# FNet layer with an MLP beside it on one Trainium2 core: bank-freeing work right behind each product, all else later, two sums of C per step, buffers and pools moved

## The chip, the cores and the metric

The kernel runs on one core of a Trainium2 chip. The metric is device time of one execution in microseconds (us). TensorE (PE) multiplies matrices into PSUM banks; VectorE (DVE) and ScalarE (ACT) read PSUM and do elementwise work; GpSimd (POOL) reduces over partitions and starts accumulating transfers; SyncE (SP) starts the other transfers. Each engine works through its own queue of instructions in order.

## The reference

```python
xn = (x - mean(x)) / sqrt(var(x) + 1e-5)                  # x: 2048 x 576, over the last axis
a, b = xn @ dft_hid_re.T, xn @ dft_hid_im.T
fnet = dft_seq_re @ a - dft_seq_im @ b                    # 2048 x 2048 by 2048 x 576, twice
mlp = maximum(xn @ w1, 0) @ w2                            # 576 x 4608 and 4608 x 576
out = x + fnet + mlp
```

## The kernel before

All matmuls are f16, with each f32 operand split into a high and a low f16 part (`split`, L182 on ScalarE for the high part and L183 on VectorE for the low one), so that one f32 product costs three f16 ones. Many products follow a seven-product scheme for a 2 x 2 block multiplication: sums and differences of blocks are formed first, then seven block products are accumulated and combined.

The hidden width of the MLP, 4608, is cut into nine blocks `b` of 512, and the 2048 rows into four groups `g` of 512. The main loop runs over the steps (b, g), numbered n from 2 to 35, blocks outermost. In a step the first matrix product of (b, g) stands among the seven parts of the second product (`mlp2`) of the step before. Blocks 0 and 1 compute the first product plainly (`mlp1_step`). From block 2 on (n = 8 to 35) it is itself done by seven products P1, P2, P6, P5, P7, P3, P4, for two pairs `first` and `second` (`pair_products`). They go through four PSUM banks: `u` of each pair, and `v` and `w` that both pairs share. P1, P6, P7 and P4 follow each other in `u`, P2 is in `v`, P5 and P3 are in `w`; P6, P7, P4 and P3 accumulate onto what their bank holds. Before the next product may write to a bank, `behind` must have read it: c11 = copy of P1 (ScalarE, L449), c11 += P2 (VectorE, L451), s1 = copy of P6 (ScalarE, L454), c22 = copy of P5 (ScalarE, L456), c22 += P7 (L458), r21 = P3 + s1 (L461). The rest makes the operands of the next step: `value` (relu on ScalarE, L444, and its low part on VectorE, L445), the relu of r21 (L462), four sums on VectorE (L463 to L468), and `end_hi` and `end_lo` (L474, L477), which split these sums and are called later through the list `ends`.

The seven parts of `mlp2` use two PSUM buffers. Parts 0, 2, 3 and 6 leave through a ScalarE copy into one of three sum buffers (`sumbufs`, L515), parts 1, 4 and 5 are added on VectorE (L517), and parts 1, 4, 5 and 6 go to memory by an accumulating transfer that GpSimd starts (L519, `spill`). In the last block two of these buffers' places are needed for the DFT's weights, so from its second step on three buffers lie in one w2 tile (`sums`).

Other work is spread over the steps by lists. `todo` holds the preparation of the next block's weights (`prepare_block`): load, largest value, scale, splits and sums, with empty entries as waits; `work()` takes one entry, and the code of a step calls it at fixed places. `passes` holds 65 entries that load a 512 KB piece of the sequence DFT matrix C (`first_c`, L863, into the one buffer `first`) and sum its absolute values on ScalarE (`sum_c`, L870), which gives the scales of C for the last stage. `tq` makes sums of x for the seven products (`sums_x`, L402 to L411), through a temporary `t` that shares the buffer `first`; so the passes begin after block 1.

After the loop, `dft1` multiplies by the hidden DFT for 16 row tiles (L989 and L999 into the banks `pd`, then L1009 to L1021), and the last stage multiplies by C (L1103), whose pieces are loaded by `load_c` (L1029) and split by `operand`. Their buffers lie in pools (`ra`, `tp`, `cs`, `cra`) that are stacked in the memory that the loop's pools have left, so where a pool stands decides which earlier tile it must wait for.

The program is written in a tile framework. It puts in the semaphores, and its scheduler sets the order of each engine's instructions from the order of the code, the dependences and its own estimate of when each can start. TensorE keeps the order of the code here; ScalarE, VectorE and the queues may take an instruction ahead of others that the code has earlier.

Of the kernel before, what the change touches and what calls it, by code (L numbers as in the profile page):

```python
# [9 lines left out]
F16 = mybir.dt.float16  # L10
# [21 lines left out]
KT = 5  # L32
# [17 lines left out]
def kernel(  # L50
# [340 lines left out]
    def sums_x(g):  # L391

        f = mlp.tile([P, 2, 2, GH], F32, tag="first", name=f"t{g}", bufs=1)
        tt = nc.vector.tensor_tensor
        for q, (head, tail) in enumerate((
            ((0, 1), (0, 0)), ((1, 1), None), ((1, 0), None), ((1, 1), (0, 1)),
        )):
            t = f[:, q % 2]
            h, l = halves(g, head)
            if tail:  # L400
                h2, l2 = halves(g, tail)
                tt(t, h, h2, ALU.subtract)  # L402
                tt(t, t, l2, ALU.subtract)
            else:
                tt(t, h, f[:, 1 - q % 2], ALU.subtract)
            tt(t, t, l, ALU.add)
# [8 lines left out]
    def pair_products(b, g, i):  # L415
# [26 lines left out]
        def value(q, src):  # L442
            hi, lo = h[:, 0, q], h[:, 1, q]
            nc.scalar.activation(hi, src, AF.Relu)  # L444
            stt(lo, src, 0.0, hi, ALU.max, ALU.subtract)  # L445

        def behind(n):
            if n == P1:
                nc.scalar.activation(c11, u, AF.Copy)  # L449
            elif n == P2:  # L450
                tt(c11, v, c11, ALU.add)  # L451
                value(A11, c11)
            elif n == P6:
                nc.scalar.activation(s1, u, AF.Copy)  # L454
            elif n == P5:
                nc.scalar.activation(c22, w, AF.Copy)  # L456
            elif n == P7:
                tt(c22, u, c22, ALU.add)  # L458
                value(A22, c22)
            elif n == P3:  # L460
                tt(r21, w, s1, ALU.add)  # L461
                nc.scalar.activation(r21, r21, AF.Relu)  # L462
                stt(s3, c11, 0.0, r21, ALU.max, ALU.subtract)  # L463
                stt(s1, c22, 0.0, r21, ALU.max, ALU.add)
                stt(s2, c22, 0.0, s3, ALU.max, ALU.subtract)
            elif n == P4:
                value(A12, u)
                stt(s4, u, 0.0, s2, ALU.max, ALU.subtract)  # L468
                ends.extend((end_hi, end_lo))

# [7 lines left out]

        def run(n):
            product(n)  # L480
            behind(n)

# [395 lines left out]
    for n in range(2, len(steps)):  # L878
# [13 lines left out]
        if b == 0 and g + 1 < NG:  # L892
            with tc.issue_after(order["lo"]):
                weave(stats([(g + 1) * TG + i for i in range(TG)]))
        if b == NB - 1 and g == 1:

            w = mlp.tile([P, 2, 7, EH], F16, tag="w2s", name="sums", bufs=4)
            w = w.rearrange("p n q e -> p (n q e)").bitcast(F32)
            sumbufs[:] = [
                w[:, k * 2 * EH : (k + 1) * 2 * EH].rearrange("p (c e) -> p c e", e=EH) for k in range(3)  # L900
            ]
        if b >= BB:
            first, second = (pair_products(b, g, i) for i in range(NQ))
            m = lambda q: mlp2(pb, pg, q)
            for k, (do, q) in enumerate((
                (first, P1), (first, P2), (m, 0), (first, P5), (first, P6), (m, 1), (second, P1),
                (first, P7), (m, 2), (second, P2), (first, P3), (first, P4), (m, 3), (second, P6),
                (m, 4), (second, P5), (second, P7), (m, 5), (m, 6), (second, P3), (second, P4),
            )):
                do(q)  # L910

                if k in (2, 4, 12, 14) and ends:
                    ends.pop(0)()
                for _ in range({2: 1, 3: 1, 5: 1, 8: 1, 9: 1, 12: 1, 13: 1, 16: 1, 18: 2}.get(k, 0)):
                    work()
                if n == 2 + NG * BB - 2 and k in (5, 9, 13, 18):
                    next(tq, None)
# [170 lines left out]
    for n, (p, kh) in enumerate(units):  # L1088
# [4 lines left out]
        for i, (q, rq, first, row, col) in enumerate(PRODUCTS):  # L1093
# [16 lines left out]
            if kh and i in (2, 4, 5, 6):  # L1110
# [3 lines left out]
                nc.sync.dma_start(out[rows, e], outs[p][:, h, e])  # L1114
    for pool in (op, cr[1], *rpool[:0:-1], cr[0], cs, tpool, rpool[0], psd, ps1):
        pool.release()
# [52 lines left out]
```

## Time and profile before

| | before |
|---|---|
| median of 3 runs (lowest, highest) | 1322.42 us (1322.38, 1323.62) |
| profiled execution, as timed | 1322.13 us |
| its span, first to last instruction | 1320.3 us |
| mean granted TensorE clock | 0.990 |
| TensorE busy | 1252.5 us (95%) |
| VectorE busy | 999.3 us (76%) |
| ScalarE busy | 726.7 us (55%) |
| GpSimd busy | 148.2 us (11%) |

The stages, read from the timeline: the start and block 0 until about 120 us, block 1 until 214, the seven-product blocks 2 to 8 from 214 to 863, the rest of `mlp2` until 875, `dft1` until about 990, and the product with C until the end. In a row of the timeline the first number is the start and the second the duration in us; a bracket at its end names how long the engine stood idle before it and what ended that. In a row of groups stand the count, the busy us, the mean ns of one, and the idle us before them. PEld is the loading of weights into TensorE. A tile is named by its buffer: `bank` is a product's PSUM bank, `acc` the place of c11 and c22, `s` the sums, `f` the piece of C.

### The profile page before, as it was taken

To read this page: it belongs to the slowest core of one execution; us is meant where nothing else is said; L and a number is where in the kernel's file an instruction comes from. 1 tells how busy PE (TensorE), PEld (TensorE's weight loads), DVE (VectorE), ACT (ScalarE), POOL (GpSimd) and SP (SyncE) were. 2 spreads that over 40 slices of the span, in tenths; PEclk is the share of its full clock that TensorE was granted. 3 is DMA by queue.
4 is the path that set the end of the run, shared out by engine and by line. 5 is a ranking of instruction groups with operands and counts; after the bars stand their busy time and mean duration, and the time that the engine had idled before them with its cause. 6 is when DMAs were issued, how large, how long until landed. Compare 5 with 4: busy or idle time off the path is not lost.

```text
span 1320.3 us, 25521 instructions
## 1 busy us (share of the span) xinstructions
PE 1252.5 (95%) x10396; PEld 994.1 (75%) x10396; DVE 999.3 (76%) x1879; ACT 726.7 (55%) x1218; POOL 148.2 (11%) x188
## 2 busy tenths in 40 slices
PE   8899998999999999899999898999999999999998
PEld 7665665877778778778778787877777777777777
DVE  8989996787677677668766767539667878878875
ACT  5745555586676667676665756435443433343332
POOL 2310021111111111121111121110000000000000
PEclk8899999999999999999999999999999999999999
DMA  5112354466656566475666665360005344343420
GB/s 220 41 64 74 110 92 91 82 134 150 146 133 145 128 143 135 110 167 126 132 140 156 145 139 120 61 127 17 1 27 190 112 148 138 108 150 113 147 82 19
DMA packets 60806, 150.75 MB, mean 114 GB/s; under 512 B 6288, under 2 KB 21136, under 8 KB 60688
## 3 DMA queue, kind: packets, MB, share of 16 engines
q1 hardware_dynamic: 42256, 111.36, 26.4%
q0 software_dynamic: 18432, 37.76, 19.3%
q8 instruction: 81, 1.33, 0.4%
q14 instruction: 37, 0.30, 0.1%
HBM read 101.91 MB, written 47.19 MB: 113 GB/s over the span
## 4 chain that ended last, share of the span: by engine, by line
PE 52%; DVE 10%; DMA 10%; issue 9%; ACT 8%; POOL 1%; SPq 0%; ACTq 0%; POOLq 0%; DVEq 0%
PE p L1103 24%; PE p L506 10%; PE bank L437 9%; PE pd L989 6%; DMA f<-in_cim_dram 4%; DMA f<-in_cre_dram 3%; ACT f L870 3%; PE p L310 2%; DVE w2s L183 2%; DMA raw_w<-in_w_dram 1%; POOL spill L519 1%; DMA c<-in_cre_dram 1%; ACT h L474 1%; DVE h L445 1%; ACT j L600 1%
## 5 line engine op out<-in xcount | busy, mean ns | idle before, releaser
L506 PE MATMUL p<-w2s,h 128*128 128x288 f16 x3024 | 409.9, 288 | 7.6 <-DVE acc L517 1.7
L506 PEld LDWEIGHTS <-h 128*128 128x128 f16 x3024 | 296.7, 98 | 87.4 <-issue 8.9
L1103 PE MATMUL p<-R,cs 128*128 128x288 f16 x2688 | 329.6, 286 | 1.5 <-DVE o L1109 1.5
L1103 PEld LDWEIGHTS <-cs 128*128 128x128 f16 x2688 | 263.0, 98 | 68.0 <-issue 1.7
L182 ACT ACTIVATE cs<-c,sc_c 128x1024 f16<-128x1024 f32 x112 | 128.4, 1148 | 196.1 <-PE p L1103 148.1
L437 PEld LDWEIGHTS <-w1buf 128*128 128x128 f16 x1600 | 157.5, 98 | 46.2 <-issue 24.5
L183 DVE SCALAR_TENSOR_TENSOR cs<-c,sc_c,cs 128x1024 f16<-128x1024 f32 x112 | 143.7, 1283 | 44.7 <-ACT cs L182 44.5
L437 PEld LDWEIGHTS <-dbuf 128*128 128x128 f16 x1200 | 117.3, 98 | 35.6 <-issue 20.2
L437 PE MATMUL bank<-acc,w1buf 128*128 128x256 f16 x768 | 106.1, 275 | 21.2 <-ACT s L454 19.6
L437 PE MATMUL bank<-xT,w1buf 128*128 128x256 f16 x832 | 110.9, 274 | 0.7 <-ACT acc L456 0.7
L989 PE MATMUL pd<-dbuf,xT 128*128 128x288 f16 x832 | 104.3, 286 | 1.7 <-DVE R L1018 1.5
L519 POOL DMA_DIRECT2D spill<-dbuf x74 | 64.7, 885 | 328.4 <-DVE dbuf L517 256.2
L989 PEld LDWEIGHTS <-xT 128*128 128x128 f16 x832 | 80.7, 98 | 25.7 <-issue 5.6
L437 PE MATMUL bank<-acc,dbuf 128*128 128x256 f16 x576 | 78.5, 272 | 17.9 <-ACT s L454 12.6
L870 ACT ACTIVATE f<-f 128x1024 f32<-128x1024 f32 x64 | 67.2, 1050 | 43.3 <-DMA f<-in_cim_dram 22.5
L477 DVE TENSOR_TENSOR h<-s,h 128x1024 f16<-128x1024 f32 x56 | 68.6, 1224 | 26.9 <-ACT h L474 26.7
L437 PE MATMUL bank<-xT,dbuf 128*128 128x256 f16 x624 | 82.3, 273 | 0.0
L474 ACT ACTIVATE h<-s 128x1024 f16<-128x1024 f32 x56 | 59.1, 1055 | 34.9 <-DVE s L468 34.9
L444 ACT ACTIVATE h<-acc 128x256 f16<-128x256 f32 x112 | 45.9, 410 | 51.6 <-DVE acc L458 33.6
L1109 DVE SCALAR_TENSOR_TENSOR o<-p,us_c,o 128x288 f32<-128x288 f32 x112 | 57.5, 514 | 19.9 <-PE p L1103 19.9
L515 ACT ACTIVATE dbuf<-p,c_ub 128x576 f32<-128x576 f32 x74 | 54.1, 732 | 22.6 <-PE p L506 17.6
L445 DVE SCALAR_TENSOR_TENSOR h<-acc,h 128x256 f16<-128x256 f32 x112 | 47.3, 422 | 23.1 <-ACT h L444 23.1
(158 smaller groups left out, 1543.1 us busy)
## 6 DMA issues: line engine op xcount, KB each, us to landing
spill<-dbuf POOLq DMA_DIRECT2D x74, 288.0 KB, 5.9
f<-in_cre_dram SPq DMA_DIRECT2D x32, 512.0 KB, 4.8
f<-in_cim_dram SPq DMA_DIRECT2D x32, 512.0 KB, 4.5
c<-in_cre_dram SPq DMA_DIRECT2D x32, 512.0 KB, 4.4
c<-in_cim_dram SPq DMA_DIRECT2D x32, 512.0 KB, 4.8
spill<-sum POOLq DMA_DIRECT2D x38, 288.0 KB, 5.5
raw_w<-in_w_dram SPq DMA_DIRECT2D x17, 640.0 KB, 5.7
raw_w<-in_w_dram SPq DMA_DIRECT2D x18, 576.0 KB, 4.0
```

Source lines behind the costliest of these rows:

```text
L182: nc.scalar.activation(hi, src, AF.Copy, scale=s)
L183: nc.vector.scalar_tensor_tensor(lo, src, s, hi, ALU.mult, ALU.subtract)
L437: nc.tensor.matmul(ps, l, r, start=first and m == 0, stop=m == len(todo) - 1, skip_group_check=not first,)
L445: stt(lo, src, 0.0, hi, ALU.max, ALU.subtract)
L474: order["s"] = nc.scalar.activation(hi_s, st[:, 1:], AF.Copy).ins
L477: order["lo"] = nc.vector.tensor_tensor(lo_s, st[:, 1:], hi_s, ALU.subtract).ins
L506: nc.tensor.matmul(ps[:, c], h[:, x, qa, c * P : (c + 1) * P], w[:, y, qb], start=first and i == 0 and j == 0, stop=i == NQ - 1 and j == 2 ...
L519: nc.gpsimd.dma_start(spill[g, row, col], o, accum_op=ALU.add)
L870: nc.scalar.activation(f, f, AF.Abs, scale=2.0**-10, accum_out=sums_c[:, n, q : q + 1])
L989: nc.tensor.matmul(ps[j], xT[g][:, kx, c * P : (c + 1) * P], dsp[j][:, hl, k], start=(t % 2 == 0 and n == 0), stop=(t % 2 == 1 and n == le ...
L1103: nc.tensor.matmul(ps, w[:, a, k], r[:, c, rq], start=first and k == 0 and j == 0, stop=k == HK - 1 and j == 2, skip_group_check=not first,)
L1109: nc.vector.scalar_tensor_tensor(o, ps, us["c"][:, n : n + 1], o, ALU.mult, ALU.add)
```

## The change

Within a step of blocks 2 to 8, `behind` is cut in two: `free` holds, for each product, the one instruction that empties its bank, and is issued right behind the product; `use` holds the rest and is issued at a place of its own, later (`later1`, `later2`). The four sums on VectorE, two of which stood behind P3, all come behind P4. P6 goes ahead of P5 in the first pair, and part 5 ahead of P7 in the second. The calls of `work()`, `ends` and `passes` get places in the same list; there are still ten calls of `work()` per step.

Each step from n = 4 on takes two entries of `passes`, in block 1 too, where blocks 2 to 8 before took two or three. So that they can start earlier, the temporaries of `sums_x` move from the buffer `first` to the ends of the weight buffers of odd blocks. Block 1 calls `work()` ten times per step instead of eight, and the preparation of blocks 2 to 8 has three empty entries in each of two places instead of two. From the third step of the last block on, the sum buffers are four, in the two buffers of `raw`, instead of three in a w2 tile. The pools are stacked in the order `ra`, `cra`, `cs`, `tp` instead of `ra`, `tp`, `cs`, `cra`.

```diff
 def sums_x(g):
-        f = mlp.tile([P, 2, 2, GH], F32, tag="first", name=f"t{g}", bufs=1)
+        f = [
+            w[:, 2 * KT * P :][:, : 2 * GH].rearrange("p (k t) -> p k t", t=GH) for w in w1bufs[2:]
+        ]
...
-        def behind(n):
-            if n == P1:
-                nc.scalar.activation(c11, u, AF.Copy)
-            elif n == P2:
-                tt(c11, v, c11, ALU.add)
-                value(A11, c11)
...
+        def end_s():
+            stt(s3, c11, 0.0, r21, ALU.max, ALU.subtract)
+            stt(s1, c22, 0.0, r21, ALU.max, ALU.add)
+            stt(s2, c22, 0.0, s3, ALU.max, ALU.subtract)
+            stt(s4, u, 0.0, s2, ALU.max, ALU.subtract)
...
+        free = {
+            P1: lambda: nc.scalar.activation(c11, u, AF.Copy),
+            P2: lambda: tt(c11, v, c11, ALU.add),
+            P6: lambda: nc.scalar.activation(s1, u, AF.Copy),
+            P5: lambda: nc.scalar.activation(c22, w, AF.Copy),
+            P7: lambda: tt(c22, u, c22, ALU.add),
+            P3: lambda: tt(r21, w, s1, ALU.add),
+        }
+        use = {
+            P2: lambda: value(A11, c11),
+            P7: lambda: value(A22, c22),
+            P3: lambda: nc.scalar.activation(r21, r21, AF.Relu),
+            P4: lambda: (value(A12, u), end_s(), ends.extend((end_hi, end_lo))),
+        }
...
     def prepare_block(b):
-        wait = [lambda: None] * 2
+        wait = [lambda: None] * (2 if b < BB else 3)
...
-        if b == NB - 1 and g == 1:
...
+        if b == NB - 1 and g:
+            size = 2 * EH
+            if g == 1:
+                w = mlp.tile([P, 2, 7, EH], F16, tag="w2s", name="sums", bufs=4)
+                w = [w.rearrange("p n q e -> p (n q e)").bitcast(F32)]
+            elif g == 2:
+                w = [raw.tile([P, KT, EH], F32, tag="raw", name=f"sums{k}") for k in range(2)]
+                w = [r.rearrange("p k e -> p (k e)") for r in w]
...
-            for k, (do, q) in enumerate((
-                (first, P1), (first, P2), (m, 0), (first, P5), (first, P6), (m, 1), (second, P1),
-                (first, P7), (m, 2), (second, P2), (first, P3), (first, P4), (m, 3), (second, P6),
-                (m, 4), (second, P5), (second, P7), (m, 5), (m, 6), (second, P3), (second, P4),
-            )):
...
-                if n > NG * BB and (k in (9, 18) or k == 14 and n % 2) and passes:
-                    passes.pop(0)()
+            count = lambda q: n > 3 and passes and passes.pop(0)()
+            for do, q in (
+                (first, P1), (first, P2), (m, 0), (end, 0), (first, P6), (ready, 1),
+                (first, P5), (later1, P2), (ready, 1), (m, 1), (end, 0), (second, P1), (ready, 1),
+                (first, P7), (m, 2), (second, P2), (later1, P7), (ready, 1),
+                (first, P3), (first, P4), (count, 0), (later1, P3), (m, 3), (later1, P4), (second, P6),
+                (later2, P2), (ready, 1), (m, 4), (end, 0), (second, P5), (ready, 1), (m, 5), (end, 0),
+                (second, P7), (ready, 1), (m, 6), (ready, 2), (second, P3), (later2, P7),
+                (count, 0), (second, P4), (later2, P3), (later2, P4), (ready, 1),
+            ):
                 do(q)
...
-            for _ in range(1 if b else 3):
+            for _ in range(1 + i % 2 if b else 3):
                 work()
+            if n > 3 and i % 2 and passes:
+                passes.pop(0)()
...
     rpool = [tc.alloc_tile_pool(name="ra", bufs=1)]
+    cr = [tc.alloc_tile_pool(name="cra", bufs=1)]
+    cs = tc.alloc_tile_pool(name="cs", bufs=4)
     tpool = tc.alloc_tile_pool(name="tp", bufs=2)
-    cs = tc.alloc_tile_pool(name="cs", bufs=4)
-    cr = [tc.alloc_tile_pool(name="cra", bufs=1)]
```

More of the change, by code (lines that the diff above doesn't have):

```diff
@@ L477, in end_lo, with run @@
             order["lo"] = nc.vector.tensor_tensor(lo_s, st[:, 1:], hi_s, ALU.subtract).ins
-        def run(n):
+        free = {
[12 more added lines that the diff above has]
+        }
+        def run(n, used=False):
+            if used:
+                return use[n]()
             product(n)
-            behind(n)
+            if n in free:
+                free[n]()
         return run
@@ L903 @@
             first, second = (pair_products(b, g, i) for i in range(NQ))
+            later1, later2 = (lambda q, f=f: f(q, True) for f in (first, second))
             m = lambda q: mlp2(pb, pg, q)
[L905 to L919 removed]
+            end = lambda q: ends and ends.pop(0)()
+            ready = lambda q: [work() for _ in range(q)]
+            count = lambda q: n > 3 and passes and passes.pop(0)()
[8 more added lines that the diff above has]
+            ):
+                do(q)
+            for _ in range(4):
+                next(tq, None)
             continue
```

28 lines of the change are left out of this document (5 added, 23 removed).

## The prediction

> **What bounds the kernel now.** I read the page's head, then the busy time by stage, then TensorE's waits, then the timelines of ScalarE and VectorE in front of the longest of them. All sums below are made against the profiled execution: a span of 1320.3 us, and 1322.13 us as timed, so 1.83 us lie around the span. That execution is 0.29 us under the median of the three runs (1322.42).
>
> ```profile
> span 1320.3 us, 25521 instructions
> ```
>
> The table by stretch (us of the stretch, then busy us and instructions of PE, PEld, DVE, ACT, POOL, the granted TensorE clock, the DMA share, GB/s):
>
> ```profile
> 200.00:240.00 40.00, 34.89 (x258) 25.71 (x257) 25.59 (x53) 20.48 (x35) 5.62 (x8) 0.96 0.38 71
> 600.00:680.00 80.00, 76.71 (x649) 64.07 (x648) 55.79 (x123) 53.51 (x104) 14.09 (x18) 0.98 0.62 139
> 800.00:840.00 40.00, 35.13 (x277) 28.05 (x275) 24.90 (x60) 21.16 (x40) 5.16 (x8) 0.91 0.45 89
> 214.00:863.00 649.00, 605.74 (x5159) 506.99 (x5158) 456.77 (x1010) 425.74 (x825) 106.30 (x136) 0.99 0.61 131
> ```
>
> The last row is the stage that the change rewrites, the 28 steps of blocks 2 to 8. TensorE is busy for 605.74 of 649 us, VectorE for 457, ScalarE for 426: TensorE sets the time, and it stands still for 43.3 us. Its waits in that stage (us in total, times, longest):
>
> ```profile
> PE bank L437 <- ACT s L454: 32.2, 20, 5.1
> PE bank L437 <- ACT acc L449: 6.7, 6, 1.7
> PE p L506 <- DVE sum L517: 1.5, 2, 0.8
> PE p L506 <- DVE dbuf L517: 1.5, 2, 0.8
> PE bank L437 <- ACT acc L456: 0.7, 1, 0.7
> ```
>
> These five make 42.6 us, and 39.6 us of it are ScalarE's three copies that empty a bank (s, c11, c22). The copies are short; they are late. A typical case, ScalarE first, then TensorE's product P7:
>
> ```profile
> 545.34 1.06 ACT L870 ACTIVATE f<-f 128x1024 f32<-128x1024 f32 x1
> 546.30 0.19 ACT L870 ACTIVATION_READ_ACCUMULATOR f<-f 128x1 f32 x1
> 546.40 0.36 ACT L456 ACTIVATE acc<-bank 128x256 f32<-128x256 f32 x1
> 546.66 0.38 ACT L454 ACTIVATE s<-bank 128x256 f32<-128x256 f32 x1
> ```
> ```profile
> 547.09 0.82 PE L437 MATMUL bank<-acc,dbuf 128*128 128x256 f16 x6 [2.10 <-ACT s L454]
> ```
>
> A sum of C (L870), which no product waits for, stands ahead of the copy that P7 waits for. Such a sum itself waits for its transfer, since there is one buffer and the next load starts only when the sum before has read it; the chain of waits shows the longest:
>
> ```profile
> 532.40 7.52 DMA f<-in_cre_dram
> ```
>
> The three longest waits of TensorE, and what ScalarE was held by before the first and the third:
>
> ```profile
> 226.32 1.44 PE L437 MATMUL bank<-acc,w1buf 128*128 128x256 f16 x6 [5.11 <-ACT s L454]
> ```
> ```profile
> 638.28 0.96 PE L437 MATMUL bank<-acc,w1buf 128*128 128x256 f16 x6 [2.18 <-ACT s L454]
> ```
> ```profile
> 824.21 1.44 PE L437 MATMUL bank<-acc,w1buf 128*128 128x256 f16 x6 [3.97 <-ACT s L454]
> ```
> ```profile
> 221.31 1.27 ACT L574 ACTIVATE dbuf<-raw_w 128x1280 f16<-128x1280 f32 x1 [3.54 <-DMA raw_w<-in_w_dram]
> ```
> ```profile
> 821.61 0.74 ACT L515 ACTIVATE sums<-p,c_ub 128x576 f32<-128x576 f32 x1 [3.40 <-DMA spill<-sums]
> ```
>
> **Part 1, the order inside a step.** Matrix pace, from the chain of waits:
>
> ```profile
> 501.38 1.47 PE p L506 x12
> 502.85 2.62 PE bank L437 x24
> ```
>
> Twelve matmuls of an mlp2 part take 1.47 us; one of a product takes 2.62/24 = 0.109, so P1, P6, P7 (6 each) take 0.66 and the others (8 each) 0.87. With the new order and no wait, counted from the step's start, TensorE ends P1 at 0.66, P2 1.53, part 0 at 3.00, P6 3.65, P5 4.53, part 1 at 6.00, the second pair's P1 6.65; then P7 is due. Later: second P6 ends 13.5, second P5 15.9, part 5 at 17.3, second P7 18.0, part 6 at 19.5, second P3 20.3, second P4 21.2. ScalarE's prices:
>
> ```profile
> L515 ACT ACTIVATE dbuf<-p,c_ub 128x576 f32<-128x576 f32 x74 | 54.1, 732 | 22.6 <-PE p L506 17.6
> ```
> ```profile
> L474 ACT ACTIVATE h<-s 128x1024 f16<-128x1024 f32 x56 | 59.1, 1055 | 34.9 <-DVE s L468 34.9
> ```
>
> In the built order of ScalarE, a sum of C stood within three instructions ahead of the first pair's s copy in 24 of 28 steps, and a sum of w1 in one more; after the change in 3 and in none. The first pair's s copy now follows part 0's copy (0.73, from 3.0), in many steps the hi of the last step's sums (1.06) or a split. In the plain step it ends near 3.0+0.73+1.06+0.38 = 5.2, with a weight split ahead, of the same 576 columns as part 0's copy and so about the same 0.73, 5.9; P7 needs it at 6.65. The 32.2 us mostly go.
>
> What is late next: the sums of C now stand ahead of two other copies. The second pair's c11 copy is wanted at 12.9 (second P6) and can run at about 7.7: 5 us of room. The second pair's c22 copy comes behind the other sum, at about 15.1 to 17.8, and is wanted at 19.5: with 1.06 for the sum and 0.36 for the copy, room of 1.3 us in the tightest step, the one in which a sum of the next block's w1 (1.27 and its read) goes ahead as well. The c11 copy of the next step's P1 has less than 1 us there by the same counting. On VectorE the sums behind P3 now all come behind P4 (four); their reader, part 2 of the next step, starts at 7.3, and the built order still has the lo of those sums ahead of part 1's addition. So this costs nothing while VectorE keeps up (457 of 649 us busy).
>
> **Part 2, two sums of C per step, and from block 1 on.** As many as before, 64. They stand about 10 us apart in every step (the first ends near 8.0, the second is due near 16.5). Before, two of the three places in the odd steps had only two parts and two products between them, 0.87+1.47+0.66+1.47 = 4.5 us. Against that, transfers land in:
>
> ```profile
> spill<-dbuf POOLq DMA_DIRECT2D x74, 288.0 KB, 5.9
> f<-in_cre_dram SPq DMA_DIRECT2D x32, 512.0 KB, 4.8
> ```
> ```profile
> raw_w<-in_w_dram SPq DMA_DIRECT2D x17, 640.0 KB, 5.7
> ```
>
> so most waits of ScalarE for f go too. Eight or so sums move into block 1; ScalarE is busy half of the time there, and I cost them at nothing (cover gone: 8 x 1.06 = 8 us at most, less whatever TensorE does not wait for). SP's queue carries each load in turn; a weight load that waits for its buffer now stands ahead of an f load that could not start before 17.8 anyway. Where f and a weight load run side by side I take 2 us more on the weight's 5.7, which eats the 1.3 us of room and leaves 0.4 us, in six steps.
>
> Residual waits of the stage: 2.4 us from that, 2 us from part 0's copy, whose sum buffer comes free with a spill that lands only about when it is wanted, 3 us where block 1 ends and ScalarE still waits for block 3's weights, 1.5 us elsewhere: 9 us, where 43.3 were. Bounds: 2 us, and 23 us (all 10.4 us that the other four rows show stay, and half of what L454 has besides its 5.11 and 3.97). Gain 34.3.
>
> **Part 3, the clock.** 0.04 x 40 + 0.02 x 80 + 0.09 x 40 = 1.6 + 1.6 + 3.6 = 6.8 us of matrix time were lost to a lower granted clock, each time right behind one of the three long waits. Block 2's preparation now ends inside block 1 (38 entries in 40 turns, before 36 in 32) and the last block has four sum buffers from its third step on instead of three, so the 5.11 and 3.97 should fall below 3 us: gain 5.2, and 1.6 stays, since a wait of 2.18 us was also followed by slow clock here. [...]
>
> **Part 4, pools moved.** At the passage to the DFT:
>
> ```profile
> 881.79 0.50 ACT L1009 ACTIVATE c<-pd,c_rho 128x288 f32<-128x288 f32 x1 [5.91 <-DMA spill<-sums]
> 885.89 1.15 ACT L182 ACTIVATE cs<-c,sc_c 128x1024 f16<-128x1024 f32 x1 [3.60 <-DMA c<-in_cre_dram]
> ```
> ```profile
> 882.13 0.33 SPq L1029 DMA_DIRECT2D c<-in_cre_dram  x1
> ```
> ```profile
> 889.27 7.01 PE L989 MATMUL pd<-dbuf,xT 128*128 128x288 f16 x51 [1.46 <-DVE R L1018]
> ```
> ```profile
> 898.27 0.28 PE L999 MATMUL pd<-dbuf,xT 64*128 64x288 f16 x1 [1.28 <-DVE R L1018]
> ```
>
> The first load of C waited for the last spill of the sums, ScalarE for that load, and TensorE 2.7 us for what ScalarE did next. In the changed program the load waits for the last matmul of mlp2 instead (about 875), some 7 us earlier, and is there before the DFT's first bank is ready at 881. The split of C now stands ahead of c12 on ScalarE; landing 3.7 us after 875 it ends by 880. Gain 2.7; were the load still at 882, the loss would be about 3.
>
> **Part 5, sums of x.** Their temporaries move into a region that block 0 still uses, so the five that ran early go later. First and last of the five, and the wait of TensorE in which they lay:
>
> ```profile
> 31.16 0.88 DVE L402 TENSOR_TENSOR t<-xT 128x512 f32<-128x512 f16 x1 [0.35 <-ACT xT L265]
> ```
> ```profile
> 36.00 0.68 DVE L406 TENSOR_TENSOR t<-t,xT 128x512 f32<-128x512 f32 x1
> ```
> ```profile
> 35.42 0.16 PE L166 MATMUL pm<-top,ones 1*128 1x2 bf16 x1 [2.85 <-DVE top L163]
> ```
> ```profile
> 120.00:160.00 40.00, 39.19 (x250) 23.41 (x248) 38.77 (x76) 20.29 (x32) 1.91 (x3) 1.00 0.32 102
> ```
>
> At most 2.85 us are gained; but they come back where VectorE is busy 38.77 of 40 us and TensorE 39.19. I take a gain of 1.0, between 2.85 and a loss of 2.5.
>
> **The sum.** 1320.3 - 34.3 - 5.2 - 2.7 - 1.0 = 1277.1; with 1.83 around it 1278.9, on the median of the runs 1279.2. I say 1279.
>
> **Rivals.** (a) Half gain: the waits move to c22 and c11 behind the sums of C; 23 us stay, the clock gives back 3 only: 1320.3 - 20.3 - 3 - 2.7 - 0 = 1294.3, timed 1296. For it: the 1.3 us of room, 7.52 us transfers; against: 10 us spacing. (b) The clock is not lowered by any wait that is left, since none reaches the length of the two long ones: 1.6 less, 1277. [...] (c) Slower: ScalarE waits for f in front of c22 in every step. TensorE loses what exceeds 1.3 us; to eat 43.2 us of gains (besides the 9 counted) in 28 steps takes 1.5 us each, so a wait of 2.8 us beyond the 8.5 us (8.0 to 16.5) that a load has: it decides if f lands more than 11.3 us after the sum before it. Then 1322 and more, 1330 at 11.6 (28 x 0.3 more). Against: 4.8 in the middle, 7.52 at the longest. (d) No change: the new program order is undone by the scheduler, 1322; against it the 24 of 28 that become 3.
>
> **Numbers.** Forecast 0.70, (a) 0.15, (b) 0.08, (c) 0.04, (d) 0.03. Faster is the first three, 0.93; within 0.2% (2.6 us, about what a measurement of this kernel can tell from no change) 0.03; slower 0.04. Range: below, the bound of 2 us of waits and 2.85 us at the start, 1279 - 7 - 1.9 - 1.6 = 1268; above, the 23 us (14 more), part 5's loss (3.5 more) and the clock of (a) (2.2 more): 1299.
>
> **What would show it.** Right: TensorE idle under 15 us between blocks 2 and 8, no row of L454's copy above 5 us in total, granted clock 0.99 or more in each 40 us there, the first load of C within 2 us of the last mlp2. Wrong: c22's or c11's copy leading TensorE's waits, or ScalarE's wait for f as long as before.

## The result, and the profile after

| | before | after |
|---|---|---|
| median of four runs each (lowest, highest) | 1322.40 us (1318.31, 1323.62) | 1284.22 us (1282.20, 1285.60) |
| profiled execution, as timed | 1322.13 us | 1285.60 us |
| its span | 1320.3 us | 1283.8 us |
| mean granted TensorE clock | 0.990 | 0.995 |

The ratio is 0.9715, with a 95% interval of 0.969 to 0.974: 38 us less. The forecast was 1279, so 5 us of the expected gain are missing. The profiled execution of the changed kernel is the slowest of its four; its span is 36.5 us shorter than before.

The busy time by stretch of the changed kernel, columns as before. The stage of blocks 2 to 8 now begins with TensorE's first product at 216.3 us (214.4 before) and ends with the last at 826.1 (862.8 before):

```profile
200.00:240.00 40.00, 39.22 (x304) 29.63 (x303) 29.67 (x62) 27.40 (x53) 7.68 (x10) 1.00 0.68 150
600.00:680.00 80.00, 78.17 (x673) 65.61 (x672) 60.75 (x134) 56.68 (x110) 14.06 (x18) 1.00 0.63 126
800.00:840.00 40.00, 40.00 (x339) 32.79 (x337) 21.25 (x44) 19.05 (x36) 9.94 (x12) 1.00 0.62 109
840.00:880.00 40.00, 37.64 (x299) 28.09 (x297) 30.61 (x48) 19.04 (x29) 0.00 (x0) 0.96 0.27 79
216.00:826.00 610.00, 598.69 (x5156) 504.02 (x5155) 457.96 (x1002) 417.83 (x808) 106.39 (x135) 1.00 0.64 132
```

The last row answers to the one of 649 us: TensorE stands still for 610 - 598.7 = 11.3 us of the stage where it stood 43.3, and the clock column is 1.00 throughout. The stage is 609.8 us long instead of 648.4, 38.6 less: 32 us of waits and 6.6 us of matrix time, about the 6.8 us that the lower clock had cost. What TensorE still waits for in the stage (us in total, times, longest):

```profile
PE bank L440 <- DVE acc L470: 4.0, 8, 1.4
PE bank L440 <- ACT acc L469: 3.5, 5, 1.1
PE bank L440 <- ACT s L468: 2.2, 3, 1.2
PE bank L440 <- DVE s L471: 1.0, 1, 1.0
```

The s copy (L468, before L454) has fallen from 32.2 us to 2.2. The group of the sums of C (count, busy us, mean ns, then the idle us ahead of them), first before, then after, and below it the transfers after (KB each, median us to landing):

```profile
L870 ACT ACTIVATE f<-f 128x1024 f32<-128x1024 f32 x64 | 67.2, 1050 | 43.3 <-DMA f<-in_cim_dram 22.5 <-DMA f<-in_cre_dram 20.4
```
```profile
L874 ACT ACTIVATE f<-f 128x1024 f32<-128x1024 f32 x64 | 67.1, 1049 | 5.1 <-DMA f<-in_cre_dram 5.1
```
```profile
spill<-dbuf POOLq DMA_DIRECT2D x74, 288.0 KB, 5.2
f<-in_cre_dram SPq DMA_DIRECT2D x32, 512.0 KB, 4.5
```

ScalarE waits 5.1 us for pieces of C in the whole program; the same group before had 43.3 us (that TensorE's idle time in the stage was also 43.3 us is chance), which points to the transfer and not to the order alone. The two transfers shown are hardly faster (spills 5.9 us before, pieces of C 4.8).

At the passage to the DFT, first SP, then ScalarE, then TensorE:

```profile
837.80 0.33 SPq L1042 DMA_DIRECT2D c<-in_cre_dram  x1
...
844.40 1.15 ACT L182 ACTIVATE cs<-c,sc_c 128x1024 f16<-128x1024 f32 x1 [5.89 <-DMA c<-in_cre_dram]
845.46 0.48 ACT L1022 ACTIVATE c<-pd,c_rho 128x288 f32<-128x288 f32 x1
...
850.89 0.28 PE L1002 MATMUL pd<-dbuf,xT 128*128 128x288 f16 x1 [0.45 <-DVE R L1031]
851.74 0.28 PE L1002 MATMUL pd<-dbuf,xT 128*128 128x288 f16 x1 [0.57 <-DVE R L1031]
853.36 7.83 PE L1002 MATMUL pd<-dbuf,xT 128*128 128x288 f16 x49 [1.34 <-DVE R L1031]
```

The load is issued 0.2 us behind the last matmul of mlp2 (837.6), as forecast, and still nothing is gained: it lands after 6.6 us, the split of C holds up the copies of the first DFT bank behind it, TensorE waits 2.4 us (2.7 before), and the clock is 0.96 in the 40 us around it, where at the passage before (880 to 920 us) it was 1.00.

### The profile page after: what moved, and what is told of

Same layout as the page of the kernel before. It is cut to its first block, busy times and chain, and to the rows that moved or that the text cites. A ratio compares the mean times of both kernels' runs of the same rounds, so it can differ in the third digit from the quotient of the medians.

```text
span 1283.8 us, 25483 instructions
## 1 busy us (share of the span) xinstructions
PE 1247.0 (97%) x10396; PEld 990.4 (77%) x10396; DVE 1002.9 (78%) x1879; ACT 727.8 (57%) x1218; POOL 149.0 (12%) x188
## 4 chain that ended last, share of the span: by engine, by line
PE 69%; DVE 17%; ACT 5%; DMA 5%; issue 3%; SPq 1%; POOL 0%; ACTq 0%; POOLq 0%; DVEq 0%
PE p L1116 25%; PE p L510 17%; PE bank L440 17%; PE pd L1002 7%; DMA raw_w<-in_w_dram 2%; DVE w2s L183 2%; PE p L310 2%; ACT h L459 1%; DVE h L448 1%; DVE h L462 1%; ACT f L874 1%; DMA c<-in_cim_dram 1%; DMA c<-in_cre_dram 1%; DVE dbuf L183 1%; DVE w1buf L183 1%
## 5 line engine op out<-in xcount | busy, mean ns | idle before, releaser
L440 PE MATMUL bank<-acc,w1buf 128*128 128x256 f16 x768 | 102.1, 272 | 4.6 <-DVE acc L470 2.9
L519 ACT ACTIVATE dbuf<-p,c_ub 128x576 f32<-128x576 f32 x74 | 54.1, 732 | 21.4 <-ACT h L447 11.3
```

What stands on the lines that cost most here:

```text
L440: nc.tensor.matmul(ps, l, r, start=first and m == 0, stop=m == len(todo) - 1, skip_group_check=not first,)
```

## The experiments

Ratios are to runs of the kernel before on the same chip, with 95% intervals; line numbers differ from kernel to kernel. The medians of the kernel before lay between 1320.0 and 1323.1 us in these series.

### The old order with the even spacing

The changed kernel, with `behind` and the list of the step as they were before:

```diff
-        free = {
...
+        def behind(n):
...
-                (first, P1), (first, P2), (m, 0), (end, 0), (first, P6), (ready, 1),
...
+                (first, P1), (first, P2), (m, 0), (first, P5), (first, P6), (m, 1), (second, P1),
...
+                if n > 3 and k in (9, 18) and passes:
+                    passes.pop(0)()
```

> The changed kernel with the old order inside a step (the copies and sums behind a product all at once, P5 ahead of P6, part 5 behind P7); two sums of C per step from block 1 on, the buffers and the pools stay as changed. In the built order of ScalarE a sum of C stands within three instructions ahead of the first pair's s copy in 20 of 28 steps (24 before the change, 3 after it). Theory, that the order made the gain: most of the 32.2 us of TensorE's waits for the s copy come back, some 20 us in all above the 10.7 us that the changed kernel has, and some slow clock: 1284 + 20 to 30, so 1304 to 1314. Rival, that the even spacing made it (a sum of C no longer waits for its transfer, which takes 4.8 us in the middle): the s copy then comes only 1.06 us later and fits into its slack: 1284 to 1290.

Measured: 1304.0 us, ratio 0.987 (0.984 to 0.990), the low end of the order theory. Nearly half of the gain is there. TensorE's longest sum of waits, and the group of the sums of C:

```profile
PE bank L440 <- ACT s L457: 16.5, 13, 3.5
```
```profile
L873 ACT ACTIVATE f<-f 128x1024 f32<-128x1024 f32 x64 | 67.0, 1046 | 3.7 <-DMA f<-in_cre_dram 3.3 <-DMA f<-in_cim_dram 0.4
```

So ScalarE's wait for C is nearly gone (3.7 us of 43.3) in the old order too, and the waits for the s copy have fallen by 15.7 us. Not all of this comes from the spacing: 9.1 us of it are the two waits of 5.11 and 3.97 us, which stood behind a weight load and a spill; at the same places the s copy costs TensorE at most 0.25 us here. Around the first, ScalarE now reads the weights some 9 us earlier, before the stage begins (at 216.0 here):

```profile
215.18 1.26 ACT L577 ACTIVATE dbuf<-raw_w 128x1280 f16<-128x1280 f32 x1
```

The second such read was at 224.37 before. This goes with the changes to block 1's `work()` calls and to the preparation, and the last block has its four sum buffers here; neither edit was tried alone in the old order. So about 7 us of the s copy's waits are left for the spacing to have taken away. In the longest of those that remain another transfer stands where C's stood, that of the next block's w1:

```profile
570.85 1.27 ACT L577 ACTIVATE dbuf<-raw_w 128x1280 f16<-128x1280 f32 x1 [3.16 <-DMA raw_w<-in_w_dram]
...
573.06 0.36 ACT L457 ACTIVATE s<-bank 128x256 f32<-128x256 f32 x1
```

### The new order with the old spacing

The kernel before, with `free`, `use` and the list of the change; in the list the sums of C keep their old number and start:

```diff
-            count = lambda q: n > 3 and passes and passes.pop(0)()
+            count = lambda q: n > NG * BB and (q < 2 or n % 2) and passes and passes.pop(0)()
...
-                (later2, P2), (ready, 1), (m, 4), (end, 0), (second, P5), (ready, 1), (m, 5), (end, 0),
+                (later2, P2), (ready, 1), (m, 4), (end, 0), (count, 2), (second, P5), (ready, 1), (m, 5), (end, 0),
```

> The kernel before with the new order inside a step and nothing else of the change: sums of C as before (from block 2 on, three in the odd steps, the third behind part 4), three sum buffers in the last block, the old pools, the old place of the temporaries of the sums of x. A sum of C stands within three instructions ahead of the first pair's s copy in 1 of 28 steps. Theory, the order: TensorE's waits in blocks 2 to 8 fall from 43.3 us to 12 to 20 (the third sum of the odd steps has 4.5 us to the next one while a transfer takes 4.8, so some waits for f stay and now meet the second pair's copies), 1290 to 1300. Rival, the spacing: the waits only move to c11 and c22 and 30 us or more of them stay, 1310 to 1320.

Measured: 1334.4 us, ratio 1.011 (1.008 to 1.014): slower than the kernel before, and outside both expectations. The order by itself loses 14 us, and ScalarE's wait for C is no shorter than before (49.7 us). Its waits, and the timeline of the longest of them (ScalarE, then TensorE; L463 is the c11 copy, L465 the s copy):

```profile
PE bank L437 <- ACT acc L463: 29.7, 12, 4.3
PE bank L437 <- DVE s L451: 5.0, 5, 1.0
PE bank L437 <- ACT s L465: 4.6, 2, 2.5
```
```profile
353.55 0.72 ACT L516 ACTIVATE dbuf<-p,c_ub 128x576 f32<-128x576 f32 x1
359.82 1.06 ACT L871 ACTIVATE f<-f 128x1024 f32<-128x1024 f32 x1 [5.55 <-DMA f<-in_cre_dram]
...
361.44 0.37 ACT L463 ACTIVATE acc<-bank 128x256 f32<-128x256 f32 x1
...
361.87 2.72 PE L437 MATMUL bank<-acc,dbuf 128*128 128x256 f16 x12 [4.26 <-ACT acc L463]
```

The s copy is free, as the order intends, and the c11 copy of the second pair has taken its place: 29.7 us where the s copy had 32.2. The piece of C was issued at 351.76, right behind the sum before it, and landed 8.0 us later, beside a weight load issued 1.4 us earlier; the sum was due at 354.3. A wait of 5.55 us is longer than the room that the prediction counted for any of the copies (5 us at most). In the trace the c11 copy of 0.37 us stood behind the sum's 5.55.

### The old order with no transfer to wait for

The kernel before, with one load of C in the loop:

```diff
     def first_c(m):
+        if m:
+            firsts[m] = firsts[0]
+            return
...
-        f = firsts.pop(m)
+        f = firsts[0]
```

> The kernel before with one load of C in the loop instead of 64: every sum of C reads the same first piece, at its old place, so that none of them waits for a transfer (left out: the other 63 loads, so the scales of C are those of one piece). Theory in the prediction's words, that the copies are late because a sum of C that itself waits for its transfer stands ahead of them: with the transfers gone, the sum's own 1.06 us is most of what is left, and the s copy needs at most about 1 us of slack; the 43.3 us fall to 12 to 20, so 1322 - 25 to 33 = 1289 to 1297. Rival, that the place alone costs the time and the transfer does not matter: over 35 us of waits stay, 1314 or more.

Measured: 1284.1 us, ratio 0.972 (0.969 to 0.976): as fast as the whole change, with the old order, the old places, the old buffers and pools, and 5 us below the range that the theory gave.

```profile
PE bank L437 <- ACT s L454: 11.0, 9, 4.7
```

The rival is excluded: the place of the sums costs little where they don't wait. Leaving out the loads also unburdens the other transfers, but that is the smaller part: ScalarE's waits in the stage for transfers other than C were 8.6 us before and are 6.3 here, against 42.9 us for C. Of the 11.0 us one wait, at 225.6, has 4.7, the one behind the weight load, which no load of C caused; the other eight stay under 1 us.

### The new order with no transfer to wait for

The same edit in the kernel with the new order and the old spacing:

> The kernel before with the new order inside a step (alone 1334) and one load of C in the loop instead of 64, all sums reading the same piece (with the old order 1284; left out: the other 63 loads, so the scales of C are those of one piece). Theory now: ScalarE's wait for the transfer is what costs, and where it stands decides only which copy it makes late. Without it the new order is as good as the old one or a little better: 1275 to 1285, and the 29.7 us of waits for the c11 copy fall below 3. Rival, that the new order with three sums in the odd steps is bad of itself: the c11 or c22 copies keep 10 us or more, 1295 or above.

Measured: 1287.3 us, ratio 0.973 (0.970 to 0.976), 2 us above the expected range. The waits for the c11 copy are gone from the list, which is led by a VectorE sum with 5.0 us. By the medians the transfers are worth 47 us here and 36 in the old order; without them the two orders cannot be told apart. With no wait for C neither is better: the order decides which copy stands behind the wait.

### The sums of C twice

The changed kernel, with

```diff
-            nc.scalar.activation(
-                f, f, AF.Abs, scale=2.0**-10, accum_out=sums_c[:, n, q : q + 1]
-            )
+            for _ in range(2):
+                nc.scalar.activation(
+                    f, f, AF.Abs, scale=1.0 if _ else 2.0**-10, accum_out=sums_c[:, n, q : q + 1]
+                )
```

> The changed kernel with every sum of C done twice in a row by ScalarE (1.06 and a read of 0.19 us more, 64 times, 80 us of ScalarE in all; the second reading has the same values up to the scale, so the scales of C differ). It tries the room that the prediction counted in the new order: 5 us ahead of the second pair's c11 copy, 1.3 us ahead of its c22 copy in the tightest step. Theory: 1.25 us more fit in nearly everywhere, only the c22 copy of some steps comes late by up to 0.6 us: 3 to 8 us more, 1287 to 1292. Rival, that the room is used up: each step loses 1 us or more at c22, so 28 us and more, 1312 or above.

Measured: 1302.5 us, ratio 0.985 (0.982 to 0.988), 18 us more than the change and between the two expectations. And it is not c22 that came late. TensorE's longest wait, ScalarE's, and the spills, all in the stage alone:

```profile
PE bank L440 <- ACT s L468: 17.3, 17, 3.0
```
```profile
ACT dbuf L519 <- DMA spill<-dbuf: 18.5, 14, 2.4
```
```profile
spill<-dbuf POOLq DMA_DIRECT2D x68, 288.0 KB, 6.5
```

Spills land in 6.5 us; in the same stretch of the changed kernel it is 5.3. So part 0's copy waits for its sum buffer, and the s copy stands behind part 0's. The room at c22 was enough; the room at the sum buffers, to which the prediction gave 2 us, is the next limit.

### A sum of C behind the c22 copy

A sum of C is issued after `order["s"]`. The edit is made in the version with both edits of the last section of the experiments:

```diff
-            P5: lambda: nc.scalar.activation(c22, w, AF.Copy),
+            P5: lambda: order.update(s=nc.scalar.activation(c22, w, AF.Copy).ins),
```

> The version with the first group's sums of x early and the first operands of C split late (1279.8), and in it each sum of C issued behind the last c22 copy instead of the last hi of the sums, so that in the built order a sum of C stands within three instructions ahead of the second pair's c22 copy in 0 of 28 steps (27 before this edit). Theory: TensorE's waits for the c22 copy (2.9 us) go, the sum has room behind it: 1276 to 1278. Rival, that the wait only moves to the next step's first c11 copy, which had less than 1 us of room by the prediction's counting: 1280 or more.

Measured: 1286.6 us, ratio 0.973 (0.971 to 0.975): 7 us slower than the version it starts from. TensorE's waits for c22 went as expected, and came back elsewhere. Below are TensorE's longest wait in the stage, the spills there, and one case on ScalarE's timeline (L473 is the s copy):

```profile
PE bank L445 <- ACT s L473: 11.1, 15, 1.5
```
```profile
spill<-dbuf POOLq DMA_DIRECT2D x67, 288.0 KB, 6.3
```
```profile
637.59 0.74 ACT L524 ACTIVATE dbuf<-p,c_ub 128x576 f32<-128x576 f32 x1 [2.12 <-DMA spill<-dbuf]
638.23 1.05 ACT L464 ACTIVATE h<-s 128x1024 f16<-128x1024 f32 x1
639.17 0.37 ACT L473 ACTIVATE s<-bank 128x256 f32<-128x256 f32 x1
```

Neither expectation had this. The load of the next piece now starts beside the step's spills (630.26 against 629.83 here), and the spills become late. Whether that is so, or the later sum alone does it, the same kernel without the loads tells:

> The version of the run before (each sum of C behind the last c22 copy, 1286.6) with one load of C in the loop instead of 64 (left out: the other 63 loads, so the scales of C are those of one piece). In that version ScalarE's copy of part 0 waited 19.2 us for spills, whose median landing rose from 5.3 to 6.3 us, and the s copy behind it cost TensorE 11.1 us. Theory: the load of C, which there starts beside the last spills of a step, slows them; without it they land in 4.7 us or less (as with the old order and no loads), the s copy's waits fall below 3 us, 1275 to 1279. Rival, that the sum of C itself, now a few us later, delays the copies of the spilled sums: spills of 4.7 us or less change little, 8 us or more of the waits stay, 1283 or more.

Measured: 1277.5 us, ratio 0.968 (0.965 to 0.970).

```profile
PE bank L445 <- ACT s L473: 3.5, 6, 0.8
```
```profile
spill<-dbuf POOLq DMA_DIRECT2D x67, 288.0 KB, 4.6
```

The spills land in 4.6 us and the s copy's waits fall to 3.5 us (under 3 was expected). So it is the loads of C that make the spills late, not the later sum. The difference is also what these loads still cost in that version: 7 us by the ratios.

### The pools as before

The changed kernel, with

```diff
-    cr = [tc.alloc_tile_pool(name="cra", bufs=1)]
-    cs = tc.alloc_tile_pool(name="cs", bufs=4)
     tpool = tc.alloc_tile_pool(name="tp", bufs=2)
+    cs = tc.alloc_tile_pool(name="cs", bufs=4)
+    cr = [tc.alloc_tile_pool(name="cra", bufs=1)]
```

> The changed kernel with the pools of the DFT stacked as before (ra, tp, cs, cra): the first load of C then waits for the last spill of the sums instead of the last matmul of mlp2. Theory of the prediction (the move is worth 2.7 us): 1286.9. Rival, that the move brought nothing, since the load is there earlier but the transfer takes 6.6 us beside the last spills instead of 3.7, and TensorE stands still 2.4 us at the passage as before (2.7): 1283 to 1285.

Measured: 1282.1 us, ratio 0.971 (0.968 to 0.973), not to be told from the change. The first load of C is issued at the same place, right behind the last matmul of mlp2 (835.46, the DFT's matmuls beginning at 835.23), and TensorE's waits at the passage are the same to the digit:

```profile
PE pd L1002 <- DVE R L1031: 2.4, 3, 1.3
```

The order of the pools is therefore not what moved the load.

### The sum buffers of the last block as before

The changed kernel, with

```diff
-        if b == NB - 1 and g:
+        if b == NB - 1 and g == 1:
...
-                w = [raw.tile([P, KT, EH], F32, tag="raw", name=f"sums{k}") for k in range(2)]
...
+                w[:, k * 2 * EH : (k + 1) * 2 * EH].rearrange("p (c e) -> p c e", e=EH) for k in range(3)
```

> The changed kernel with three sum buffers in one w2 tile through the whole last block, as before the change, instead of four in the two weight buffers from its third step on. Theory: the first load of C waits for the last spill again (before: issued 7 us behind the last matmul of mlp2, not 0.2 us), so the passage costs some 3 to 5 us more, and ScalarE waits for a spill in the last block again (3.4 us before, with 3.97 us for TensorE and 3.6 us of slow clock behind it): 1287 to 1293. Rival, that in the new order such a wait of ScalarE falls into slack and the load has time: 1284 to 1285.

Measured: 1285.9 us, ratio 0.972 (0.970 to 0.975): no measurable loss. This edit does move the load, to 845.29, 7.4 us behind the last matmul of mlp2, as before the change. Yet TensorE's wait at the passage is not longer:

```profile
845.29 0.33 SPq L1036 DMA_DIRECT2D c<-in_cre_dram  x1
...
844.88 0.50 ACT L1016 ACTIVATE c<-pd,c_rho 128x288 f32<-128x288 f32 x1 [6.07 <-DMA spill<-sums]
...
852.49 8.68 PE L996 MATMUL pd<-dbuf,xT 128*128 128x288 f16 x51 [1.75 <-DVE R L1025]
```

Here the first copy waits for a spill, there it waited for a load; the end is the same. And in the last block the spill that is late again (2.2 us on ScalarE) costs TensorE 0.5 us instead of 3.97.

### The first splits of C later, the first sums of x earlier

The changed kernel with each of two edits, and with both. The first:

```diff
-        nc.scalar.activation(hi, T, AF.Copy)
+        r = nc.scalar.activation(hi, T, AF.Copy).ins
+        if t == 3:
+            order["r"] = r
...
-        split(w[:, 0], w[:, 1], src, sc["c"][:, n : n + 1])
+        with tc.issue_after(order["r"]) if m < 3 else nullcontext():
+            split(w[:, 0], w[:, 1], src, sc["c"][:, n : n + 1])
```

> The changed kernel with the first three operands of C split only behind the copies of the DFT's row tile 3, so that ScalarE does not wait for the first load of C ahead of the first bank's copies. Theory, that ScalarE's wait of 5.9 us for this load is what TensorE's 2.4 us at the passage follow from: they go, and the 1.6 us that the lower clock of 0.96 behind them cost: 1280.2. Rival, that the first row tile's copies are late in any case, since they overwrite memory that the last spills still read (the last is issued at 838.8 and lands 6.2 us later): over 1.5 us of waits stay, 1283 to 1284.

Measured: 1281.8 us, ratio 0.970 (0.967 to 0.972). The profile gives each theory half: the split no longer stands ahead, but the copy behind it now waits for the last spill, and 1.28 us of TensorE's 2.4 stay; the clock does not drop (1.00 between 840 and 880 us).

```profile
847.40 0.89 ACT L1030 ACTIVATE R<-pd,c_rho 128x288 f16<-128x288 f32 x2 [4.54 <-DMA spill<-sums]
...
850.91 6.16 PE L1002 MATMUL pd<-dbuf,xT 128*128 128x288 f16 x49 [1.28 <-DVE R L1031]
```

The second:

```diff
+        if g == 0:
+            f = mlp.tile([P, 2, 2, GH], F32, tag="first", name="t0", bufs=1)
+            f = [f[:, q] for q in range(2)]
+        else:
```

> The changed kernel with the temporary of the first group's sums of x back in the buffer of the pieces of C (free until the first piece is loaded), so that these sums can run early again, as before the change; the other groups' temporaries stay where the change put them. In the trace of the changed kernel TensorE was 2.0 us ahead of before at 41 us, had lost that by 80 us, and fell 1.3 us back between 118 and 206 us, while VectorE was busy 39.8 of 40 us. Theory, that the late sums of x cost the 1.3 us or more in block 1: 1282 to 1283, and some of the 2 us at 41 us are lost again. Rival, that the eight sums of C and the two more entries of the weights' preparation per step cost it: no change, 1284.

Measured: 1283.8 us, ratio 0.971 (0.969 to 0.973): no measurable change, as the rival had it. Which of the rival's two causes it would be was not tried.

> The two edits of the runs before the last taken together: the first group's sums of x early, and the first three operands of C split behind row tile 3. If both theories hold: 1284.2 - 1.5 - 4.0 = 1278.7. If neither does: 1284.

Measured: 1279.8 us (1278.6 to 1280.5), ratio 0.968 (0.966 to 0.970). It is the fastest complete kernel here. All five of its runs lie below all four of the version with only the sums of x early (1281.6 to 1285.8, same chip), so the late split gives something there; against the changed kernel, which was not run beside it, the intervals of the ratios overlap by 0.1%.

The start of block 2 shows how far such a small term can be read. In the four kernels with the old front part it lies between 214.2 and 214.7 us; in five of the six with the changed one between 215.7 and 216.3, but at 214.2 in the one with the old pools; in three of the four with early sums of x between 214.8 and 215.2, but at 216.2 in the one that has nothing else. A loss of some 1.5 us at the front by the change, half of which the early sums give back, is likely and not shown; up to 2 us belong to the single execution.

## Why the prediction was right, and where it was off

The forecast of 1279 (range 1268 to 1299) was 5 us low, and the direction right. Its terms against the two profiled executions:

| term, us of span | forecast | found |
|---|---|---|
| waits in blocks 2 to 8 | 34.3 | 32.0 (43.3 to 11.3) |
| clock in blocks 2 to 8 | 5.2 | 6.6 (matrix time) |
| first load of C, with all behind the stage | 2.7 | -0.2 |
| sums of x, start of block 2 | 1.0 | -1.9 |
| sum | 43.2 | 36.5 |

**Parts 1 and 2, the stage.** The size held: 11.3 us idle against 9, under the 15 named as the mark, no row of the s copy above 5, and the mechanism (a copy behind a sum of C that waits for its transfer) is what the rows show. That the 9 us came so close is partly luck, since its terms were off in both directions: the 3 us where block 1 ends came to nothing, and 5.0 us where 1.5 were kept for "elsewhere" are VectorE's two additions that empty a bank (L470 and L471). (The 2 us for part 0's copy held: the s copy's 2.2 us stand behind it.) L470 leads the list with 4.0 us; 1.36 us of it is one wait at 783.7, in which a split of the DFT's weights (1.72 us) stood ahead of it on VectorE. The prediction took VectorE's order to cost nothing while it keeps up. (Its upper bound of 23 us comes to 22 by its own terms, 10.4 and 11.6.)

What the prediction had wrong is also which part carries it. It wrote that the 32.2 us "mostly go" by the order, and then that by the spacing "most waits of ScalarE for f go too". The runs make it a matter of both together (medians, us):

| | old spacing | even spacing | no transfers |
|---|---|---|---|
| old order | 1322.4 | 1304.0 | 1284.1 |
| new order | 1334.4 | 1284.2 | 1287.3 |

(The even spacing has the other edits of the change with it. Of these the pools, the sum buffers and the place of the first sums of x moved nothing measurable by themselves in the new order; block 1's `work()` calls and the longer preparation were not tried alone. As said above, some 9 of the 16 us that the s copy's waits lost in the old order belong to two waits that no piece of C caused.) That the order alone is a loss has its reason in the rivals: (a) and (c) have the waits move to c22 and c11 behind the sums of C. Rival (c) named its point, a piece that lands 11.3 us after the sum before it, for the even spacing; the prediction also found 4.5 us between two places of the old spacing, and there the 8.0 us seen above are enough. The working was done for the change as a whole and not for its parts.

For c22 in the tightest step the prediction counted 1.3 us of room, and 0.4 us lost in six steps, by an estimate of 2 us more for a weight load beside a piece of C that no run shows by itself (a load of 640 KB took 5.7 us by median in the stage of the kernel before, 5.2 us in the same kernel without the loads of C): the copy costs 3.5 us in five waits of up to 1.1 us, where 2.4 were forecast. Right in place and mechanism. But the room at part 0's sum buffer, costed at 2 us, is the smaller one: two edits that load it (sums twice, sums later) brought the s copy's waits back through it, 17.3 and 11.1 us.

**Part 3, the clock.** Nearly all of the 6.8 us came back; the 1.6 us that were kept for waits near 2.2 us went too: no wait of that length is left in the stage (the longest is 1.4), and the clock is 1.00 from 216 to 826 us. That is rival (b) in its result. The mark of 3 us, below which the two long waits were to fall for the gain, was the author's estimate and no run shows it: in the kernel with only the new order the clock was 0.66 from 360 to 365 us behind a wait of 4.26 us and 1.00 behind one of 3.18 us, and it was lower behind some shorter waits, as told at the end.

**Part 4, the pools.** The step that failed is that the load "is there before the DFT's first bank is ready", "landing 3.7 us after". The landing took 6.6 us, beside the last spills and three other loads of C issued in the same 1.5 us, and then the split was in the way that the text mentions and takes for harmless. Also the edit that moved the load was that of the sum buffers and not that of the pools. And the load was not all that set the wait: with it 7.4 us later TensorE waits 1.75 us instead of 2.4. The wait itself is 0.3 us shorter than before, but the lower clock behind it costs 0.04 x 40 = 1.6 us, for which the prediction had no term.

**Part 5, the sums of x.** A gain of 1.0 was taken between 2.85 and -2.5. In the trace TensorE is 2.0 us ahead at 41 us and has lost that by 80: at 54.9 it waits 2.19 us for a ScalarE copy, before 1.62, and nine matmuls behind it take 3.68 us instead of 2.10. By 216 us it is 1.9 us behind. The bound was right, the value within it was not; how much of the 1.9 us is the change's own is not settled, as said above.

The step from the sum of 1278.9 to the 1285.6 of the profiled execution is thus 2.9 each for parts 4 and 5 and 2.3 us of waits, less 1.4 of clock. The median lies 1.4 us under that execution.

## What to carry to other kernels

An instruction that waits for a transfer delays what stands behind it on its engine (here a c11 copy of 0.37 us, behind a sum of C that waited 5.55 us), so first find how long it waits and what makes the transfer late; here an order that protects one urgent instruction only handed the wait to the next. Test the parts of such a change alone: here, by the ratios, the spacing with the other edits is worth 17 us, the order alone costs 14, and together they are worth 38. When the waits on one transfer are gone, look at the transfers beside it: a load of C that started a little later made the spills land 1 us later (6.3 us by median instead of 5.3), and their buffers became the limit.

## What was not expected of the hardware

The granted clock was lower behind waits of TensorE that were shorter than the 2.18 us of the kernel before (0.66 from 638 to 643 us there): 0.72 from 855 to 860 us behind 1.75 us at the passage in the kernel with the old sum buffers, 0.75 from 305 to 310 us behind 2.15 us at 303 us in the old order with even spacing, and 0.71 from 855 to 860 us behind the three short waits (0.45, 0.57 and 1.34 us) at the passage of the changed kernel. First the passage with the old sum buffers, where the wait ends at 852.49; then the kernel with only the new order, where waits of 4.26, 3.18 and 2.60 us end at 361.87, 455.51 and 503.14, and only behind the first the clock is lower (the granted clock is the third number from the end; behind the other two it was 1.00 in the next 5 us as well):

```profile
850.00:855.00 5.00, 2.97 (x21) 1.89 (x19) 4.35 (x7) 4.00 (x7) 0.00 (x0) 0.94 0.55 202
855.00:860.00 5.00, 5.00 (x31) 3.52 (x30) 5.00 (x9) 1.54 (x5) 0.00 (x0) 0.72 0.00 0
```
```profile
360.00:365.00 5.00, 3.13 (x16) 2.18 (x16) 2.87 (x7) 3.59 (x8) 0.00 (x0) 0.66 0.53 143
...
454.00:459.00 5.00, 3.49 (x31) 2.98 (x31) 3.22 (x7) 3.59 (x9) 0.00 (x0) 1.00 0.68 165
...
502.00:507.00 5.00, 3.86 (x34) 3.32 (x34) 3.73 (x8) 4.45 (x11) 0.49 (x2) 1.00 0.71 144
```

Length alone does not decide here. The closest pair is at the passage: 1.75 us with the old sum buffers was followed by 0.72, and 1.77 us in the version with both edits of the last section by 1.00. TensorE's row and the clock of that version:

```profile
848.84 6.16 PE L1007 MATMUL pd<-dbuf,xT 128*128 128x288 f16 x49 [1.77 <-DVE R L1036]
```
```profile
840.00:850.00 10.00, 7.83 (x64) 6.00 (x62) 5.54 (x10) 2.84 (x5) 0.00 (x0) 1.00 0.51 168
850.00:860.00 10.00, 10.00 (x86) 7.65 (x85) 7.94 (x17) 5.61 (x9) 0.00 (x0) 1.00 0.01 2
```

What decides besides the length is not shown by these runs.

Transfers of one size landed in very different times. That other transfers beside them are the cause is shown for the spills alone, by the runs without the loads of C. A 512 KB piece of C landed in 3.7 to 4.8 us by median in the kernels before and after, 8.0 once beside a weight load, and the first four pieces for the last stage of the changed kernel in 9.4 by median (6.5 to 11.3); a 288 KB spill, by median in the stage, in 4.6 us (later sums) and 4.7 us (old order) without the loads of C, 5.3 with them in the changed kernel, 6.0 in the kernel before, and 6.3 to 6.5 in the two kernels with later or doubled sums.
